# First tile's local scores ahead of its global queries' scores, its operands fetched first in pieces, exponential table loaded at the start

## The chip, the cores and the metric

The kernel runs on one core of one Trainium2 chip. Times are device microseconds (us) of one launch. Before the change the median of three runs is 953.72 us (953.09 to 955.16). The engines are named as in the profile: PE (TensorE matmuls; PEld are its weight loads), DVE (VectorE), ACT (ScalarE), POOL (GpSimd) and SP (SyncE, which here only issues DMAs).

## The reference

Attention for 8 batches of 8 heads, with 512 local and 32 global tokens of 64 dimensions, and then a feed-forward layer over all 8 x 544 rows of 512 features. Global queries see all keys. A local query sees the 32 global keys and the local keys at most 32 places away.

```python
s_g = scale * q_g @ [k_g, k_l].T;   out_g = softmax(s_g) @ [v_g, v_l]
s_ll = where(|i - j| <= 32, scale * q_l @ k_l.T, -1e9)
s_lg = scale * q_l @ k_g.T
out_l = softmax([s_lg, s_ll]) @ [v_g, v_l]
x = concat(out_g, out_l)            # 4352 rows of 512
h = x @ w_in                        # 512 x 2048
g = where(h > 0, h, exp(min(h, 0)) - 1)
out = g @ w_out                     # 2048 x 512
```

## The kernel before

Two generators are interleaved while the program is written: `attention()` and `ffn_stream()`. A third, `load_weights()`, is stepped from the same loop. What a generator writes is then ordered for each engine by a list scheduler, so the order of an engine's instructions is fixed in the program, and every engine works through its own list in order.

**Attention** goes through slots: for each batch `b` and each group `g` of four heads one slot ("g", b, g) for the global queries, and one slot ("l", b, g, t) for each of four tiles `t` of 128 local queries. In batch 0 the order is g0, its tiles 0 to 3, g1, its tiles 0 to 3. The stages of a slot are:

- `stage_ga` (L703 to L732): 16 score matmuls and four small ones of the global queries, two maxima on DVE (L715), their product with the scale (L716), the exponentials on ACT (L720 into `pg`, L722 into `pu`), and two steps later the normalization (`norm`): a sum and a reciprocal on DVE (L726 to L728), then `pk` (four pieces, L731) and `pg` (L732) on POOL.
- `stage_s` (L769 to L795): 8 score matmuls of a local tile, four mask-and-minimum operations on DVE (L780), four exponentials on ACT (L786), and their normalization, a reciprocal on DVE (L791) and four products on POOL (L793). The tile `p` is one of three buffers in turn (p_94, p_95, p_93 in the orders below).
- `stage_t` and `stage_u` (L742 to L811), three slots behind: transposes of `p` (L809), `pz`, `pk` and `pg` on PE, copied into `ptw` and `ptg` by DVE (L811, L753) and ACT (L746 to L750).
- `stage_v` (L822, L853): the products with the values, copied into `xr` by ACT (L859).

Operands are fetched by SP, two slots ahead (`loads`, `AHEAD`): `qg` and two tiles `k` of 640 KB with a "g" slot, two tiles `q` of 256 KB with the first "l" slot, and the mask `msk` behind those.

**Weights.** `unit(m, p, raw)` turns 1 MB of 64-bit weights (`raw`, two buffers, fetched at L174) into two f16 halves: L188 on ACT, L189 on POOL, L193, L196 and L200 on DVE, L204 on ACT, and, after an `all_max` over the partitions (L141, L142), L213 on ACT and L216 on DVE. L204 is the last reader of `raw` as it came; the next fetch into that buffer waits for it.

**Feed-forward.** Its first matmuls (L324) need a block's `xh` and `xl` (L568 on ACT, L571 on DVE), which need that block's whole attention output, and converted weights. Until step 66 of the attention's stages (`PACE`, `lead`) no feed-forward work is written.

At the very start `WARM` matmuls of 512 columns on zeros (L152) keep PE busy while the first operands are on their way. The ACT engine's table of the exponential is loaded where the first exponential is, ahead of L720. The slots of batch 0 before:

```python
slots += [(*a, *t) for g in range(2) for a, t in [(("g", b, g), ())] + [(("l", b, g), (t,)) for t in range(NT)]]
```

Of the kernel before, what the change touches and what calls it, by code (L numbers as in the profile page):

```python
# [10 lines left out]
F32 = mybir.dt.float32  # L11
F32R = mybir.dt.float32r
I32 = mybir.dt.int32
AF = mybir.ActivationFunctionType
# [6 lines left out]
B, H, SL, SG, D = 8, 8, 512, 32, 64  # L21
DM, DF = 512, 2048
P = 128
NT = SL // P
HQ = P // 2
KW = HQ + 3 * 32
# [10 lines left out]
AHEAD = 2  # L37


PACE = ((0, 0), (66, 0), (112, 180), (320, 850))  # L40
WARM = 10
CONV = 14
NBL = B * SL // BLK
GROUPS = {"a": (0, 1), "b": (1, 2), "c": (2, 4), "d": (4, 8), "f": (0, 8)}
# [16 lines left out]
def attn_ffn(ctx: ExitStack, tc: tile.TileContext, qT, qgT, kT, vT, vgT, vpT, w_in, w_out, mask, out):  # L61
    nc = tc.nc
# [3 lines left out]
    wts = ctx.enter_context(tc.tile_pool(name="wts", bufs=1))  # L66
    ffn = ctx.enter_context(tc.tile_pool(name="ffn", bufs=2))
    apool = ctx.enter_context(tc.tile_pool(name="att", bufs=2))
# [33 lines left out]
    msk = wts.tile([P, 3, KW], F32, name="msk")  # L102
# [47 lines left out]
    nc.vector.memset(warm, 0.0)  # L150
    for _ in range(WARM):
        nc.tensor.matmul(ps_o.tile([P, DM], F32, name="acc"), warm[:, 0:P], warm, start=True, stop=True)  # L152
    pww = wts.tile([P, NP], F32, name="pww")
    pwo = wts.tile([P, NP], F32, name="pwo")
    isc = wts.tile([P, NP], F32, name="isc")
    tab = {}

# [502 lines left out]
    def attention():  # L660
# [3 lines left out]
        def load_k(b, hp):  # L664
            k = apool.tile([P, NT, 2, KW], F32, name="k", bufs=4)
            nc.sync.dma_start(k, kT[b, hp])
            return k

        def load_q(b, hp):
            q = apool.tile([P, SL], F32, name="q", bufs=4)  # L670
            nc.sync.dma_start(q, qT[b, hp])
            return q

        def load_qg(b, g):
            qg = apool.tile([P, 2, SG], F32, name="qg", bufs=1)
            nc.sync.dma_start(qg, qgT[b, g])
            return qg
# [235 lines left out]
        slots = []  # L913
        for b in range(B):
            if b == 0:
                slots += [(*a, *t) for g in range(2) for a, t in [(("g", b, g), ())] + [(("l", b, g), (t,)) for t in range(NT)]]
                continue
            body = [("l", b, g, t) for h in range(2) for g in range(2) for t in (2 * h, 2 * h + 1)]
            slots += [("g", b, 0)] + body[:2] + [("g", b, 1)] + body[2:]
        sts = [{"b": b} for b in range(B)]  # L920
        n = len(slots)

        def loads(i):

            s = slots[i]
            st = sts[s[1]]
            if s[0] == "g":
                st["qg", s[2]] = load_qg(s[1], s[2])
                for hp in (2 * s[2], 2 * s[2] + 1):
                    st["k", hp] = load_k(s[1], hp)  # L930
            else:
                for hp in (2 * s[2], 2 * s[2] + 1):
                    if ("q", hp) not in st:
                        st["q", hp] = load_q(s[1], hp)
                if i == 1:
                    nc.sync.dma_start(msk, mask)

        for i in range(AHEAD):
            loads(i)
        def load_values(s):  # L940
            if s and s[0] == "l":
                _, b, g, t = s
                if ("vg", g) not in sts[b]:
                    sts[b]["vg", g] = load_vg(b, g)
                sts[b]["v", g, t] = load_v(b, g, t)
# [3 lines left out]
        for i in range(n + LAGT + 1):  # L949
            if i + AHEAD < n:  # L950
                loads(i + AHEAD)
# [5 lines left out]
            if i == switch:  # L957
                clear(ptw[2])
                k = turns["p"]
# [3 lines left out]
            for what in "SVTU" if i < switch else "TSUV":  # L963
# [7 lines left out]
                elif what == "V":  # L971
                    if pairs:
                        b, g, half = pairs.pop()
# [100 lines left out]
```

## Time and profile before

| | |
|---|---|
| median of three runs | 953.72 us (953.09 to 955.16) |
| the profiled execution's own time | 954.72 us |
| its span on the core | 952.9 us |
| PE / DVE / ACT / POOL busy | 908.5 / 728.1 / 670.1 / 271.1 us |

The span is what the trace covers, from the first to the last instruction. The profiled execution's own time is 1.82 us longer than its span, and 1.00 us above the median. Busy times are sums over the whole span; they are averages over a first part in which no engine is always busy and a long rest in which PE nearly always is.

### The profile page before, as it was taken

What the parts mean: (1) busy time and instruction counts of PE and PEld (TensorE: products, weight loads), DVE (VectorE), ACT (ScalarE), POOL (GpSimd) and SP (SyncE); (2) the same over time, 40 slices, a digit from 0 to 9 for tenths busy, and PEclk for the clock granted to TensorE, in tenths of its full rate; (3) what the DMA queues carried; (4) which work ended last, traced back from release to release, by engine and by line L of the source; (5) the groups of instructions that cost most, each with busy time, mean ns of one, the idle gap of its engine ahead of it and who ended that gap; (6) DMA issues with size and microseconds to landing.
All of it is one profiled execution on the core that took longest, in us unless ns stands there. A gap on an engine that the chain in (4) does not pass through costs nothing.

```text
span 952.9 us, 23830 instructions
## 1 busy us (share of the span) xinstructions
PE 908.5 (95%) x9216; PEld 727.8 (76%) x9216; DVE 728.1 (76%) x2025; ACT 670.1 (70%) x1584; POOL 271.1 (28%) x483
## 2 busy tenths in 40 slices
PE   6889887899999999999999999999999999999997
PEld 3567564566666788888888888888888888888886
DVE  4988988889967777768776877687777777676566
ACT  5888996776656767757677767677767767666564
POOL 4655481461522322122121212221332312100000
PEclk8779999899999999999999999999999999999999
DMA  6855876331342023101330123102310101000000
GB/s 262 299 179 180 282 224 191 124 123 57 115 157 90 23 100 103 47 26 46 105 121 26 46 78 125 47 27 79 122 49 25 46 23 35 2 23 23 1 24 23
DMA packets 41769, 87.64 MB, mean 92 GB/s; under 512 B 7736, under 2 KB 8888, under 8 KB 41656
## 3 DMA queue, kind: packets, MB, share of 16 engines
q1 hardware_dynamic: 41368, 85.85, 26.6%
q8 instruction: 73, 1.20, 0.5%
q14 instruction: 40, 0.33, 0.1%
q10 hardware_dynamic: 288, 0.26, 0.1%
HBM read 70.89 MB, written 15.20 MB: 90 GB/s over the span
## 4 chain that ended last, share of the span: by engine, by line
PE 67%; DVE 14%; ACT 9%; POOL 3%; issue 3%; DMA 3%; SPq 0%; DVEq 0%; ACTq 0%; POOLq 0%
PE pa L324 25%; PE acc L482 12%; PE h L482 9%; PE acc L447 4%; PE pa L822 3%; PE h L324 3%; PE pa L769 3%; PE pa L809 2%; ACT p L786 2%; DMA raw<-w_out 2%; PE pa L889 2%; DVE gl L345 1%; POOL p L793 1%; DVE cu L196 1%; DVE cu L200 1%
## 5 line engine op out<-in xcount | busy, mean ns | idle before, releaser
L324 PEld LDWEIGHTS <-winh 128*128 128x128 f16 x2160 | 209.4, 98 | 39.2 <-issue 8.4
L793 POOL TENSOR_SCALAR p<-p,sm 128x128 f32<-128x128 f32 x256 | 147.8, 593 | 303.2 <-DVE sm L791 165.0
L324 PE MATMUL pa<-xh,winh 128*128 128x256 f16 x824 | 224.9, 273 | 0.1
L324 PE MATMUL pa<-xl,winh 128*128 128x256 f16 x824 | 224.6, 273 | 0.0
L324 PE MATMUL pa<-xh,winl 128*128 128x256 f16 x824 | 224.6, 273 | 0.0
L361 ACT ACTIVATE gh<-gx,xs 128x896 f16<-128x896 f32 x103 | 107.3, 1042 | 123.1 <-DVE gx L358 123.0
L345 DVE SCALAR_TENSOR_TENSOR gl<-gx,xs,gh 128x896 f16<-128x896 f32 x103 | 119.4, 1159 | 59.9 <-ACT gh L361 59.0
L482 PEld LDWEIGHTS <-gh 128*128 128x128 f16 x1456 | 139.5, 98 | 24.0 <-issue 7.4
L786 ACT ACTIVATE p<-p,m 128x160 f32<-128x160 f32 x256 | 106.7, 421 | 41.6 <-DVE m L780 41.4
L324 PEld LDWEIGHTS <-winl 128*128 128x128 f16 x1080 | 106.1, 98 | 14.3 <-issue 1.2
L333 ACT ACTIVATE g<-pa,xs 128x512 f32<-128x512 f32 x103 | 70.3, 682 | 24.4 <-PE pa L324 23.8
L482 PE MATMUL acc<-wouth,gh 128*128 128x256 f16 x312 | 85.2, 273 | 0.0
L482 PE MATMUL acc<-woutl,gh 128*128 128x256 f16 x312 | 85.1, 273 | 0.0
L335 ACT ACTIVATE g<-g 128x512 f32<-128x512 f32 x135 | 85.0, 630 | 0.1
L482 PE MATMUL acc<-wouth,gl 128*128 128x256 f16 x312 | 85.0, 273 | 0.0
L482 PEld LDWEIGHTS <-gl 128*128 128x128 f16 x728 | 71.2, 98 | 9.2 <-DVE gl L345 1.0
L482 PE MATMUL h<-raw,gh 128*128 128x256 f16 x416 | 75.0, 273 | 0.0
L324 PE MATMUL h<-xh,winh 128*128 128x256 f16 x256 | 71.1, 279 | 1.5 <-ACT hs L334 0.9
L324 PE MATMUL h<-xl,winh 128*128 128x256 f16 x256 | 71.0, 278 | 0.7 <-DVE xl L571 0.7
L324 PE MATMUL h<-xh,winl 128*128 128x256 f16 x256 | 71.0, 278 | 0.0
L780 DVE CUSTOM_DVE_ANT_0 p<-pa,msk 128x160 f32<-128x160 f32 x228 | 61.5, 318 | 4.8 <-PE pa L769 4.7
L342 DVE SCALAR_TENSOR_TENSOR gx<-g,hs 128x512 f32<-128x512 f32 x51 | 35.9, 704 | 36.0 <-ACT g L335 35.6
(236 smaller groups left out, 2016.9 us busy)
## 6 DMA issues: line engine op xcount, KB each, us to landing
k<-kT SPq DMA_DIRECT2D x32, 640.0 KB, 5.1
v<-vT SPq DMA_DIRECT2D x64, 256.0 KB, 2.8
q<-qT SPq DMA_DIRECT2D x32, 256.0 KB, 5.6
raw<-w_in SPq DMA_DIRECT2D x8, 1024.0 KB, 5.9
raw<-w_out SPq DMA_DIRECT2D x8, 1024.0 KB, 6.8
out<-o SPq DMA_DIRECT2D x32, 256.0 KB, 2.3
od<-o SPq DMA_DIRECT2D x24, 256.0 KB, 3.1
o<-od SPq DMA_DIRECT2D x24, 256.0 KB, 2.8
```

Of the source, the lines that this page charges most:

```text
L324: nc.tensor.matmul(h[:, j, :], wt[:, c, f], xt[:, c, :], start=k == 0, stop=k == 11)
L333: nc.scalar.activation(g, hf, AF.Relu, scale=sc[:, p:p + 1])
L335: nc.scalar.activation(g, g, AF.Exp, scale=-1.0)
L342: nc.vector.scalar_tensor_tensor(out=out, in0=ins[0], scalar=-1.0, in1=ins[1], op0=ALU.add, op1=ALU.max)
L345: nc.vector.scalar_tensor_tensor(out=dst, in0=src, scalar=sg, in1=hi, op0=ALU.mult, op1=ALU.subtract)
L361: nc.scalar.activation(gh, gx, AF.Copy, scale=sg)
L447: nc.tensor.matmul(acc[t], gt[:, s], wt[:, f, :], start=p == first and j == 0 and k == 0, stop=p == last and j == 1 and k == 2)
L482: nc.tensor.matmul(cols, gt, w, start=p == 0 and k == 0, stop=last and k == len(todo) - 1, skip_group_check=True)
L769: nc.tensor.matmul(sp[r][half * HQ:(half + 1) * HQ, j * KW:(j + 1) * KW], q[rows, qs], k[rows, t, half, :], start=True, stop=True)
L780: nc.vector.tensor_tensor_reduce(out=p, in0=sp[r][:, j * KW:(j + 1) * KW], in1=msk[:, mi, :], op0=ALU.add, op1=ALU.min, scale=-scale, scal ...
L786: nc.scalar.activation(ps[i], ps[i], AF.Exp, bias=m[:, i:i + 1], scale=-1.0, accum_out=s[:, 0, i:i + 1])
L793: nc.gpsimd.tensor_scalar(ps[i][:, 0:P], ps[i][:, 0:P], s[:, 1, i:i + 1], 1.0, ALU.mult, ALU.mult)
```

## The change

The first local tile's slot of batch 0 moves ahead of the first global slot. The operands of these two slots are fetched in a new function: first only those parts of `k`, `q` and the mask that tile 0 reads (160, 64 and 80 KB), the two pieces of `q` from ACT's DMA queue instead of SP's, then `qg`, then the remaining parts. One exponential on a tile of 128 x 1 zeros is written ahead of all else on ACT, so that the table load stands there. Two of the ten warm matmuls go.

```diff
-WARM = 10
+WARM = 8
...
     pwo = wts.tile([P, NP], F32, name="pwo")
+    early = wts.tile([P, 1], F32, name="early")
+    nc.vector.memset(early, 0.0)
+    nc.scalar.activation(early, early, AF.Exp)
...
             if b == 0:
-                slots += [(*a, *t) for g in range(2) for a, t in [(("g", b, g), ())] + [(("l", b, g), (t,)) for t in range(NT)]]
+                slots += [("l", b, 0, 0), ("g", b, 0)] + [("l", b, 0, t) for t in range(1, NT)]
+                slots += [("g", b, 1)] + [("l", b, 1, t) for t in range(NT)]
                 continue
...
-                if i == 1:
-                    nc.sync.dma_start(msk, mask)
-
-        for i in range(AHEAD):
-            loads(i)
+
+        def first_loads():
+
+            st = sts[0]
+            for hp in range(2):
+                k = st["k", hp] = apool.tile([P, NT, 2, KW], F32, name="k", bufs=4)
+                q = st["q", hp] = apool.tile([P, SL], F32, name="q", bufs=4)
+                nc.sync.dma_start(k[:, 0], kT[0, hp][:, 0])
+                nc.scalar.dma_start(q[:, 0:P], qT[0, hp][:, 0:P])
+            nc.sync.dma_start(msk[:, 0, :], mask[:, 0, :])
+            st["qg", 0] = load_qg(0, 0)
+            for hp in range(2):
+                nc.sync.dma_start(st["k", hp][:, 1:], kT[0, hp][:, 1:])
+            for hp in range(2):
+                nc.sync.dma_start(st["q", hp][:, P:], qT[0, hp][:, P:])
+            nc.sync.dma_start(msk[:, 1:, :], mask[:, 1:, :])
+
+        first_loads()
```

The three lines of the table load and the new function push later lines down by 3 and more: in the orders of the changed kernel L789 is the L786 of before, L723 and L725 are L720 and L722, L191 is L188, L192 is L189, L571 is L568, L734 and L735 are L731 and L732, L796 is L793. The scheduler orders all engines anew. From the 140th of ACT's 1268 instructions and the 280th of DVE's 2027 to the end, the orders of before and of the changed kernel are the same.

The start of ACT's list, before:

```order
L720 ACT_TABLE_LOAD
L720 ACTIVATE pg,sg<-pa,mg 128x4x64 x2
L722 ACTIVATE pu,sg<-pa,mg 128x32
L786 ACTIVATE p_94,sm<-p_94,m 128x160 x4
L188 ACTIVATE cu<-raw 128x1024
L786 ACTIVATE p_95,sm<-p_95,m 128x160 x4
L786 ACTIVATE p_93,sm<-p_93,m 128x160 x2
L188 ACTIVATE cu<-raw 128x1024
```

and in the changed kernel:

```order
L947 DMA q<-qT 128x128 x2
L157 ACT_TABLE_LOAD
L157 ACTIVATE early<-early 128x1
L789 ACTIVATE p_94,sm<-p_94,m 128x160 x4
L723 ACTIVATE pg,sg<-pa,mg 128x4x64 x2
L725 ACTIVATE pu,sg<-pa,mg 128x32
L789 ACTIVATE p_95,sm<-p_95,m 128x160 x4
L789 ACTIVATE p_93,sm<-p_93,m 128x160 x2
L191 ACTIVATE cu<-raw 128x1024
```

The local tile's four exponentials stand ahead of the global queries', and the first conversion of weights (L188, now L191) behind six more local exponentials.

POOL's list behind its memsets, before:

```order
L731 TENSOR_SCALAR pk_91<-pu,sg 32x32 x4
L732 TENSOR_SCALAR pg<-pg,sg 128x512
L793 TENSOR_SCALAR p_94<-p_94,sm 128x128 x3
L189 TENSOR_SCALAR cu<-cu 128x1024
L793 TENSOR_SCALAR p_94<-p_94,sm 128x128
L189 TENSOR_SCALAR cu<-cu 128x1024
L793 TENSOR_SCALAR p_95<-p_95,sm 128x128 x4
```

and in the changed kernel:

```order
L796 TENSOR_SCALAR p_94<-p_94,sm 128x128 x4
L734 TENSOR_SCALAR pk_91<-pu,sg 32x32 x4
L735 TENSOR_SCALAR pg<-pg,sg 128x512
L796 TENSOR_SCALAR p_95<-p_95,sm 128x128 x4
L192 TENSOR_SCALAR cu<-cu 128x1024
L796 TENSOR_SCALAR p_93<-p_93,sm 128x128 x4
L192 TENSOR_SCALAR cu<-cu 128x1024
```

Tile 0 is normalized ahead of `pk` and `pg`, and each of the first two weight conversions stands behind one local tile more than before.

ACT's list at the end of the lead, before, from the last tile of group 1 on:

```order
L786 ACTIVATE p_94,sm<-p_94,m 128x160 x2
L859 COPY xr<-h 128x2x128
L786 ACTIVATE p_94,sm<-p_94,m 128x160 x2
L188 ACTIVATE cu<-raw 128x1024
L568 ACTIVATE xh<-xr,xm 128x1024
L720 ACTIVATE pg,sg<-pa,mg 128x4x64 x2
L722 ACTIVATE pu,sg<-pa,mg 128x32
```

and in the changed kernel:

```order
L789 ACTIVATE p_94,sm<-p_94,m 128x160
L571 ACTIVATE xh<-xr,xm 128x1024
L789 ACTIVATE p_94,sm<-p_94,m 128x160
L749 COPY ptw_81<-pa 64x4x32
L751 COPY ptw_81<-pa 64x4x32
L753 COPY ptg_84<-pa 128x2x64
L191 ACTIVATE cu<-raw 128x1024
L723 ACTIVATE pg,sg<-pa,mg 128x4x64 x2
```

The first block's `xh` stood behind the sixth weight conversion (L188, which reads a `raw` that has to arrive) and now stands ahead of it.

## Rows read from the trace of the kernel before

**Rows 1.** The page's first line.
```profile
span 952.9 us, 23830 instructions
```

**Rows 2.** Windows: stretch, length, busy us (count) by engine; clock, DMA share, GB/s.
```profile
10.00:15.00 5.00, 1.11 (x17) 0.78 (x13) 2.93 (x24) 4.99 (x21) 2.32 (x7) 1.00 1.05 403
15.00:20.00 5.00, 4.18 (x23) 2.20 (x23) 2.47 (x4) 3.99 (x16) 3.52 (x5) 0.53 0.68 269
20.00:25.00 5.00, 2.58 (x25) 2.24 (x25) 5.00 (x13) 1.79 (x5) 2.72 (x2) 0.50 0.20 41
250.00:300.00 50.00, 50.00 (x477) 33.94 (x479) 37.51 (x98) 31.82 (x86) 16.95 (x25) 1.00 0.32 108
```

**Rows 3.** Timeline of the first 18 us: start, length, engine, line, [idle before].
```profile
1.18 0.89 SPq L666 DMA_DIRECT2D k<-kT  x2
1.18 4.21 PE L152 MATMUL acc<-wouth 128*128 128x512 f16 x10 [1.18 <-DVE wouth L150]
...
6.84 0.63 PE L703 MATMUL pa<-k,qg 64*32 64x256 f32 x4 [0.39 <-DMA k<-kT]
...
8.76 1.28 ACT L720 ACT_TABLE_LOAD   x1 [8.76 <-DVE mg L716]
9.06 0.33 DVE L780 CUSTOM_DVE_ANT_0 p<-acc,msk 128x160 f32<-128x160 f32 x1 [0.38 <-PE acc L769]
...
10.06 0.47 ACT L720 ACTIVATE pg<-pa,mg 128x256 f32<-128x256 f32 x1
...
11.23 0.43 ACT L786 ACTIVATE p<-p,m 128x160 f32<-128x160 f32 x1
...
12.36 1.37 POOL L731 TENSOR_SCALAR pk<-pu,sg 32x32 f32<-32x32 f32 x4 [8.90 <-ACT p L786]
...
12.88 1.11 ACT L188 ACTIVATE cu<-raw 128x1024 f32<-128x1024 f32 x1
...
14.49 1.07 POOL L793 TENSOR_SCALAR p<-p,sm 128x128 f32<-128x128 f32 x3
...
15.65 1.04 POOL L189 TENSOR_SCALAR cu<-cu 128x1024 f32<-128x1024 f32 x1
...
16.72 0.69 DVE L193 TENSOR_SCALAR cu<-cu 128x1024 int32<-128x1024 int32 x1 [2.86 <-POOL cu L189]
```

**Rows 4.** DMA issues of the first 60 us: line, count, KB each, median us to landing.
```profile
qg<-qgT SPq DMA_DIRECT2D x4, 32.0 KB, 2.5
```

**Rows 5.** Timeline from 18 to 37 us, around the first two conversions of weights.
```profile
18.22 0.69 DVE L811 COPY ptw<-pa 128x512 f32<-128x512 f32 x1 [0.80 <-PE pa L809]
...
22.28 5.09 POOL L793 TENSOR_SCALAR p<-p,sm 128x128 f32<-128x128 f32 x8 [3.50 <-DVE sm L791]
...
24.96 1.16 ACT L204 ACTIVATE raw<-cu 128x1024 f32<-128x1024 f32 x1 [2.20 <-DVE cu L200]
...
26.22 0.38 SPq L174 DMA_DIRECT2D raw<-w_out  x1
...
36.23 1.16 ACT L188 ACTIVATE cu<-raw 128x1024 f32<-128x1024 f32 x1
```

**Rows 6.** Timeline from 63 to 68 us, around the sixth conversion.
```profile
63.05 0.15 DVE L136 TENSOR_SCALAR xm<-xm 128x1 int32<-128x1 int32 x1
64.60 1.13 ACT L188 ACTIVATE cu<-raw 128x1024 f32<-128x1024 f32 x1 [1.61 <-DMA raw<-w_out]
65.63 1.13 ACT L568 ACTIVATE xh<-xr,xm 128x1024 f16<-128x1024 f32 x1
66.67 0.46 ACT L720 ACTIVATE pg<-pa,mg 128x256 f32<-128x256 f32 x1
67.82 1.08 PE L809 MATMUL pa<-ident,p 128*128 128x128 f32 x4 [2.41 <-ACT pg L720]
```

**Rows 7.** Windows of the lead, columns as in rows 2.
```profile
40.00:50.00 10.00, 9.50 (x62) 6.32 (x62) 9.31 (x43) 8.07 (x28) 8.32 (x14) 0.50 0.96 344
50.00:60.00 10.00, 9.88 (x131) 6.95 (x128) 8.33 (x37) 8.42 (x34) 4.64 (x10) 0.86 0.61 192
```

## The prediction

> **What bounds the kernel now.** I read the windows over the whole span first. From 250 us on PE is busy without a gap: 50.00 of 50 us, at the full clock [rows 2]. What stands there is not touched: behind the first seventh of the lists both programs have the same order on every engine. So nothing is won or lost in the long rest; a change of the start reaches the end as a shift, the same number of microseconds at 80 us and at 952.9 us [rows 1]. No transfer in the chain is tied to an absolute time either: the weight fetches wait for buffers, and those shift along.
>
> So the question is when the lead, the first 80 us, is done. There I read the windows of the first 25 us [rows 2]. ACT has no gap from 10 to 15 us (4.99 of 5), while DVE stands half idle (2.93, then 2.47 of 5); from 20 to 25 us it is the other way round: DVE 5.00 of 5, ACT 1.79. The timeline of that stretch [rows 3] says why. ACT does nothing for 8.76 us, since its first work needs the maxima of the global queries' scores, which need 1.3 MB of keys (the landing at 6.84). Then it loads the exponential's table, 1.28 us, and only at 11.23 does the first local exponential start. DVE meanwhile has little to do, and waits 2.86 us ahead of the first weight conversion (L193 at 16.72) for POOL, which stands behind `pk`, `pg` and three products of tile 0. From there DVE, ACT and POOL take turns as the bound.
>
> **The change, part by part.**
>
> *Warm matmuls.* Eight of ten at 4.21 / 10 = 0.42 us [rows 3]: PE is free at 1.18 + 3.37 = 4.55 us. If tile 0's operands are there by then, the cover is gone and nothing is lost.
>
> *Pieces.* Before, the two tiles `k` are issued at 1.18 and the second has landed at 6.84 [rows 3]. Now tile 0 needs 2 x 160 + 2 x 64 + 80 = 528 KB instead of 1312. The smallest transfer of the trace, 32 KB, takes 2.5 us from issue to landing [rows 4]: the mask's piece, SP's third issue (0.45 us for each of the two ahead of it), is issued near 1.7 and so lands at 4.2 at best; going by the old rate, 528 of 1312 KB puts it later by up to 1 us. I take 4.6, PE's own end of the warm-up. One DMA issue more on SP, and two on ACT, lie in time in which both engines had nothing to do.
>
> *Tile 0 first.* With 1 us for its 8 matmuls and one mask operation of 0.33 + 0.08 us, ACT's first local exponential starts near 6.0 instead of 11.23. Four take 1.65 us (11.23 to 12.88 [rows 3]) and end near 7.7. The global queries' keys have 128 KB of `q` and 80 KB of mask ahead of them; of the 6.84 - 1.18 = 5.7 us from issue to landing some 2.5 are the same for any transfer [rows 4], so 1312 KB take 3.2 us and 208 KB 0.5: they land near 7.3. From landing to the maxima took 8.76 - 6.84 = 1.9 us [rows 3]; the global exponentials start near 9.2. Before they did at 10.06, behind the table load: 0.85 us earlier, of which the load gives 1.3 and the later landing takes 0.5.
>
> *The table load.* ACT had 8.76 us without work ahead of it; on the chain it costs 10.06 - 8.76 = 1.30 us [rows 3], and all of that leaves. The Trainium skill, in "ScalarE: Activation LUTs", section "What ACT_TABLE_LOAD costs", counts 1283 ns for the load and about 1380 ns for a drain, 2.66 us in all. By that the global exponentials would start 2.2 us earlier instead of 0.85. The trace has the 1.28 us of the load and an exponential right behind it, so I stay with the row.
>
> *POOL.* Its list now begins with tile 0's four products. A product takes 1.07 / 3 = 0.36 us where DVE is idle and 5.09 / 8 = 0.64 us where DVE is busy [rows 3, 5]. The reciprocal for them comes with the global maxima, near 8.9, so they end between 10.3 and 11.5. `pk` then waits for a DVE reciprocal that stands behind tile 0's copy (0.69 us [rows 5]), the transposes ahead of that, and the global exponentials: between 11.6 and 12.7, where before it was 12.36. I take 12.1. `pk` and `pg` take 14.49 - 12.36 = 2.13 us; then come four products of the next tile (1.4 to 2.5 us) where three stood: the first conversion L189 starts near 16.2 instead of 15.65, and so DVE's L193 near 17.3 instead of 16.72. So the start that was won on ACT, 5 us for the local tile, does not reach the weights: they are about 0.6 us *later*. The second conversion on POOL stands behind four products more, whose reciprocal now stands behind the first conversion on DVE. That opens a wait of some 1.5 us on DVE that it did not have (5.00 of 5 in 20 to 25 us [rows 2]): the second L204, at 24.96 before [rows 5], comes near 26.5, 1.6 us late.
>
> But more is done by then. Going down both lists to the second L200, DVE has behind it, beyond what it had before, three mask operations (0.33 each), tile 1's copy to `ptw` (0.69), 1.7 us by these rows [rows 3, 5], and two small reductions and a `pz`, which I put at half of that, an estimate: about 2.4 us. ACT has, up to the second L204, three local exponentials (1.24) and four copies more. 2.4 us of work done, 1.6 us late: **0.8 us gained**. Bounds: 2.4 if POOL's products all run at 0.36 and nothing is late; nothing at all, or a little below, if all run at 0.64.
>
> The fetch of the fourth `raw` moves to about 27.8 from 26.22; it was used at 36.23, ten us later [rows 5], so 1.6 us are covered there. Were that cover gone, the 1.6 us would be lost.
>
> *The sixth conversion.* At 62.99 ACT waits 1.61 us for `raw`, converts (64.60), then makes `xh` of the first block (65.63) and only then the global exponentials (66.67), for which PE waits 2.41 us [rows 6]. What `xh` needs was ready at 63.05 + 0.15. Now `xh` stands ahead of the wait, in time that was idle, and the exponentials follow the conversion at once: 66.67 - 65.63 = **1.04 us**. Bounds: 0, if `raw` comes so early that the order makes no difference, and 1.6.
>
> *Sum.* 0.8 + 1.04 = 1.8 us. The profiled execution goes from 954.72 to 952.9 us; it lies 1.00 above the median, so the same shift of the median gives **951.9 us**. All shorter or longer terms are bounded by 0 and 2.4 + 1.6 = 4.0 us.
>
> **The rivals.** About 0.2% (1.9 us) is what a measurement of this kernel can tell from no change.
>
> *The head start is given back.* If weights, and not DVE's or ACT's work in all, set the end of the lead, then the 2.4 us of work done early are idle later, and the 0.6 and 1.6 us of lateness count: with the 1.04 us behind them, a gain of 0 +- 0.8, 953.7 us. For it: L193 waits on POOL for 2.86 us now. Against: DVE is at 9.31 of 10 us from 40 to 50 [rows 7], where work done early is worth its time. The same time comes out if the pieces land no earlier than the whole tiles did. Chance 0.19.
>
> *More, by the clock.* From 40 to 50 us PE is granted half its clock (0.50, that is 1.2 GHz) and is busy 9.50 of 10 us [rows 7]. If the shifted work leaves it at 2.4 GHz there, DVE with 9.31 of 10 is the bound, which frees 0.7 us, and of DVE's 1.7 idle us in 50 to 60 us another 1.5, some 2.2 us in all: 1.8 + 2.2 = 4.0 us, 949.7 us. Chance 0.18.
>
> *Slower, by the clock.* PE works 9.88 of 10 us from 50 to 60 us, at 0.86 [rows 7]. If the half-clock stretch moves there, each us of it costs half a us, since PE has no slack. Eleven us, about as long as the stretch it has now, cost 5.5 us: 951.9 + 5.5 = 957.4 us. It turns the sign when it covers 3.6 us and is seen as slower from 7.4 us on. That fewer warm matmuls can start it is in the Trainium skill, "TensorE: Matmul & The Clock Gate", section "What's actually happening": the default state is throttled, and activity releases it. By that rule a later release would also put tile 0's scores and the global queries' at half speed, some 1 us of the gain. The rows bear it out in part: the warm matmuls, 0.42 us for 512 columns, run at 1.2 GHz. Chance 0.13.
>
> **How the numbers follow.** The forecast, a gain of 0.8 to 3 us (950.7 to 952.9), has 0.50; 0.27 of it lies beyond 1.9 us, 0.23 within. Faster: 0.27 + 0.18 = 0.45. Same: 0.23 + 0.18 of the first rival's 0.19, 0.41. Slower: 0.13 and the last hundredth, 0.14. The range leaves out a tenth at each end: down to 948.0 (beyond the 4.0 us of the clock rival) and up to 956.0, inside the slower rival.
>
> **What would show it.** ACT's first local exponential near 6 us; table load before 3 us; global exponentials near 9.2; L193 (now L196) at 17.3 rather than 16.7; the second L204 (now L207) near 26.5; `xh` ahead of the sixth conversion, and the first feed-forward matmul 1.8 us earlier than its place before; from there a constant shift. Wrong would be made of it by a different half-clock stretch between 40 and 75 us, or by a first conversion that is not late, so that 2 us more are won.

## The result and the profile after

The changed kernel takes 955.58 us (median of 22 runs, 952.33 to 959.27), the kernel before, run beside it, 952.31 us (22 runs, 948.46 to 958.29). The ratio of the comparison is 1.0047, 95% interval 1.0031 to 1.0063, about 4.5 us (the two medians alone lie 3.3 us apart): **slower** by half a per cent, with an interval clear of 1, where 1.8 us of gain were forecast. Single runs of one program differ by some 10 us, so a single span decides nothing here. The page of the changed kernel has a shorter span than [rows 1], because that run lay low among its own and that of before lay high:

```profile
span 951.9 us, 23838 instructions
```

So for differences late in the lead I compare two further profiles that lie at their kernels' medians, e1_before (span 949.2) and e12_after_again (953.9). Up to the first feed-forward matmul the weight conversions of the two profiles of before agree within 0.5 us, those of the two of the changed kernel within 1.6: in e12_after_again four of the first global score matmuls take 1.07 us instead of 0.63 in the first profile after, and the global exponentials start at 11.13 instead of 10.38.

The timeline of the first 18 us of the changed kernel answers to [rows 3]:

```profile
1.64 0.43 SPq L948 DMA_DIRECT2D msk<-mask  x1
1.66 1.28 ACT L157 ACT_TABLE_LOAD   x1 [1.66 <-PEq L1082]
2.12 0.43 SPq L679 DMA_DIRECT2D qg<-qgT  x1
2.59 0.91 SPq L951 DMA_DIRECT2D k<-kT  x2
...
6.00 0.43 ACT L789 ACTIVATE p<-p,m 128x160 f32<-128x160 f32 x1 [2.85 <-DVE m L783]
...
8.42 0.63 PE L706 MATMUL pa<-k,qg 64*32 64x256 f32 x4 [0.39 <-DMA k<-kT]
...
10.30 1.47 POOL L796 TENSOR_SCALAR p<-p,sm 128x128 f32<-128x128 f32 x4 [6.83 <-DVE mg L719]
10.38 0.47 ACT L723 ACTIVATE pg<-pa,mg 128x256 f32<-128x256 f32 x1 [2.62 <-PE pa L772]
...
13.16 1.36 POOL L734 TENSOR_SCALAR pk<-pu,sg 32x32 f32<-32x32 f32 x4 [1.39 <-DVE sg L731]
...
16.79 1.04 POOL L192 TENSOR_SCALAR cu<-cu 128x1024 f32<-128x1024 f32 x1
...
17.86 0.69 DVE L196 TENSOR_SCALAR cu<-cu 128x1024 int32<-128x1024 int32 x1 [0.34 <-POOL cu L192]
```

The local exponential starts at 6.00, as forecast. The rest of the keys does not land near 7.3 but at 8.42: SP issues the mask's piece at 1.64 and `qg` at 2.12, and comes to the keys' rest at 2.59, where it issued the whole tiles at 1.18 before. The global exponentials thus start at 10.38, *later* than the 10.06 of before, and POOL's list is about 0.8 us later than it was.

From 18 to 30 us (answers to [rows 5]):

```profile
20.00 2.51 POOL L796 TENSOR_SCALAR p<-p,sm 128x128 f32<-128x128 f32 x4 [2.17 <-DVE sm L794]
...
22.59 1.04 POOL L192 TENSOR_SCALAR cu<-cu 128x1024 f32<-128x1024 f32 x1
...
23.67 0.69 DVE L196 TENSOR_SCALAR cu<-cu 128x1024 int32<-128x1024 int32 x1 [1.46 <-POOL cu L192]
...
27.46 1.13 ACT L207 ACTIVATE raw<-cu 128x1024 f32<-128x1024 f32 x1 [2.29 <-DVE cu L203]
```

The wait of 1.46 us on DVE is the forecast one, but the second L207, the step that frees the buffer `raw`, comes at 27.46 instead of 24.96: 2.5 us late, not 1.6.

Windows, columns as in [rows 2]; the second and third answer to [rows 7], the last to the end of [rows 2]:

```profile
20.00:25.00 5.00, 2.43 (x11) 1.73 (x13) 3.51 (x9) 3.13 (x8) 4.83 (x7) 0.50 0.28 52
...
40.00:50.00 10.00, 7.87 (x99) 6.53 (x100) 8.67 (x38) 8.99 (x35) 5.42 (x12) 0.89 0.95 325
50.00:60.00 10.00, 7.98 (x111) 5.36 (x107) 9.99 (x47) 9.04 (x30) 5.82 (x11) 1.00 0.84 283
...
250.00:300.00 50.00, 50.00 (x495) 34.06 (x497) 37.50 (x97) 32.89 (x88) 15.88 (x25) 1.00 0.36 115
```

From 20 to 25 us POOL is now full (4.83 of 5) and DVE is not (3.51, before 5.00). From 40 to 60 us PE runs faster than before (0.89 and 1.00 against 0.50 and 0.86) and yet nothing is gained: it is busy only 7.87 and 7.98 of 10 us.

### The profile page after: what moved, and what is told of

The parts are those of the page before. It is cut to its first block, busy times and chain, and to the rows that moved or that the text cites. A ratio compares the mean times of both kernels' runs of the same rounds, so it can differ in the third digit from the quotient of the medians.

```text
span 951.9 us, 23838 instructions
## 1 busy us (share of the span) xinstructions
PE 903.6 (95%) x9214; PEld 725.6 (76%) x9214; DVE 728.4 (77%) x2026; ACT 670.7 (70%) x1585; POOL 271.1 (28%) x483
## 3 DMA queue, kind: packets, MB, share of 16 engines
q1 hardware_dynamic: 41800, 85.72, 26.7%
## 4 chain that ended last, share of the span: by engine, by line
PE 69%; DVE 13%; ACT 10%; issue 3%; DMA 2%; POOL 2%; SPq 0%; DVEq 0%; ACTq 0%; POOLq 0%
PE pa L327 25%; PE acc L485 12%; PE h L485 9%; PE acc L450 4%; PE h L327 4%; PE pa L825 4%; PE pa L772 3%; PE pa L812 3%; ACT p L789 2%; PE pa L892 2%; DVE gl L348 1%; PE pa L706 1%; ACT cu L191 1%; DVE xl L574 1%; ACT g L336 1%
## 5 line engine op out<-in xcount | busy, mean ns | idle before, releaser
L327 PEld LDWEIGHTS <-winh 128*128 128x128 f16 x2160 | 209.2, 98 | 39.4 <-issue 8.7
L796 POOL TENSOR_SCALAR p<-p,sm 128x128 f32<-128x128 f32 x256 | 143.4, 578 | 309.3 <-DVE sm L794 163.7
L327 PE MATMUL pa<-xh,winh 128*128 128x256 f16 x824 | 224.9, 273 | 0.1
L327 PE MATMUL pa<-xl,winh 128*128 128x256 f16 x824 | 224.6, 273 | 0.0
L327 PE MATMUL pa<-xh,winl 128*128 128x256 f16 x824 | 224.6, 273 | 0.0
L364 ACT ACTIVATE gh<-gx,xs 128x896 f16<-128x896 f32 x103 | 107.3, 1042 | 123.3 <-DVE gx L361 123.2
L789 ACT ACTIVATE p<-p,m 128x160 f32<-128x160 f32 x256 | 106.8, 420 | 44.5 <-DVE m L783 44.3
L327 PEld LDWEIGHTS <-winl 128*128 128x128 f16 x1080 | 106.0, 98 | 14.3 <-issue 1.3
L338 ACT ACTIVATE g<-g 128x512 f32<-128x512 f32 x135 | 85.1, 630 | 0.1
L327 PE MATMUL h<-xh,winh 128*128 128x256 f16 x256 | 70.7, 278 | 1.8 <-ACT hs L337 1.0
L327 PE MATMUL h<-xl,winh 128*128 128x256 f16 x256 | 70.9, 277 | 0.8 <-DVE xl L574 0.8
L327 PE MATMUL h<-xh,winl 128*128 128x256 f16 x256 | 70.9, 277 | 0.0
```

What stands on the lines that cost most here:

```text
L327: nc.tensor.matmul(h[:, j, :], wt[:, c, f], xt[:, c, :], start=k == 0, stop=k == 11)
L338: nc.scalar.activation(g, g, AF.Exp, scale=-1.0)
L364: nc.scalar.activation(gh, gx, AF.Copy, scale=sg)
L789: nc.scalar.activation(ps[i], ps[i], AF.Exp, bias=m[:, i:i + 1], scale=-1.0, accum_out=s[:, 0, i:i + 1])
L796: nc.gpsimd.tensor_scalar(ps[i][:, 0:P], ps[i][:, 0:P], s[:, 1, i:i + 1], 1.0, ALU.mult, ALU.mult)
```

## The experiments

Four theories stand in the expectations. **A (order):** the second weight conversion comes late, because more local-tile work stands ahead of it on POOL and ACT, and its lateness is handed on through the two buffers `raw` to the end of the lead. **B (clock):** PE is granted 1.2 GHz elsewhere, because fewer warm matmuls and different gaps lie ahead. **C (landing):** the pieces make the global keys land later, and all behind them. **D (end of the lead):** the late start is made good by 65 us and the loss arises where `xh` stands ahead of the sixth conversion.

All numbers in one place. Ratios are to the kernel before, run beside each. The starts, in us, come from one profile each: of the second and fourth release (L204, in the changed kernel L207: the step that frees a buffer `raw`), of the first feed-forward matmul (L324, L327) and of the first feed-forward activation (L335, L338), for which 24 of these matmuls must be done.

| run | median | ratio, 95% | 2nd | 4th | first L324 | first L335 |
|---|---|---|---|---|---|---|
| first profile before | 952.31 | | 25.0 | 47.4 | 77.1 | 81.1 |
| first profile after | 955.58 | 1.0047 [1.0031, 1.0063] | 27.5 | 50.4 | 78.3 | 82.2 |
| e1_before | 950.75 | 1.0003 [0.9985, 1.0020] | 24.9 | 47.9 | 76.7 | 80.7 |
| e2_table | 949.72 | 0.9996 [0.9982, 1.0009] | 25.3 | 48.2 | 76.3 | 80.2 |
| e3_oldslots | 955.58 | 1.0056 [1.0035, 1.0076] | 26.8 | 50.4 | 81.4 | 86.3 |
| e4_whole | 956.50 | 1.0061 [1.0039, 1.0082] | 29.2 | 52.0 | 80.7 | 84.7 |
| e5_warm10 | 956.17 | 1.0051 [1.0029, 1.0074] | 27.7 | 50.4 | 78.3 | 84.0 |
| e6_clamp3 | 955.23 | 1.0048 [1.0023, 1.0073] | 29.2 | 51.3 | 80.7 | 84.8 |
| e7_after_noclamp | 957.39 | 1.0073 [1.0050, 1.0096] | 25.0 | 49.5 | 79.6 | 85.3 |
| e8_before_noclamp | 958.46 | 1.0080 [1.0056, 1.0105] | 24.6 | 50.7 | 80.5 | 84.6 |
| e9_conv_first | 954.79 | 1.0049 [1.0029, 1.0069] | 27.7 | 52.0 | 81.0 | 86.4 |
| e10_conv_x | 955.73 | 1.0066 [1.0047, 1.0085] | 28.1 | 50.9 | 80.0 | 85.1 |
| e11_whole_early | 952.14 | 1.0017 [1.0001, 1.0033] | 27.4 | 49.9 | 78.7 | 82.7 |
| e12_after_again | 955.67 | 1.0053 [1.0034, 1.0073] | 28.2 | 50.8 | 78.6 | 84.2 |
| e13_copies | 952.63 | 1.0030 [1.0017, 1.0043] | 26.7 | 48.1 | 76.5 | 82.1 |
| e14_copies_dve | 950.65 | 1.0006 [0.9985, 1.0027] | 25.3 | 46.7 | 76.5 | 80.5 |
| e15_table_dve | 953.10 | 1.0023 [1.0008, 1.0038] | 24.2 | 47.6 | 77.4 | 81.4 |
| e16_copies_dve2 | 951.76 | 1.0008 [0.9992, 1.0025] | 26.2 | 48.0 | 77.5 | 81.4 |

**The two kernels again** (e1 unchanged before, e12 unchanged after):

> The kernel of before once more, for a second trace of it and for what two identical programs differ by. Theory A (order): the changed kernel is slower because the second weight conversion stands behind tile 2's products on POOL and comes 2.5 us late, which the lead never makes up; then here the second L204 stands within 0.3 us of 24.96 again, and the ratio is 1.000 within 0.002. Theory B (clock): the difference between the two programs is which stretches PE spends at half clock, and those differ by execution; then this trace has other half-clock stretches, and the start of the feed-forward stage moves by more than 1 us against the first trace.

> The changed kernel again, unchanged, beside the three above: a second profile of it, and its time on the same chip. All theories: 1.003 to 1.006 of the kernel before. If half-clock stretches near 80 and 107 us belong to its order, both profiles have them; the first has the one at 107.1 only.

The loss is there again. The two also show how lateness travels. ACT's timeline from 24 to 52 us, conversions alone, in e1_before:

```profile
24.93 1.15 ACT L204 ACTIVATE raw<-cu 128x1024 f32<-128x1024 f32 x1 [2.20 <-DVE cu L200]
...
28.60 1.13 ACT L188 ACTIVATE cu<-raw 128x1024 f32<-128x1024 f32 x1
...
37.52 1.14 ACT L204 ACTIVATE raw<-cu 128x1024 f32<-128x1024 f32 x1
...
47.91 1.15 ACT L204 ACTIVATE raw<-cu 128x1024 f32<-128x1024 f32 x1 [1.18 <-DVE cu L200]
```

and in e12_after_again:

```profile
28.21 1.16 ACT L207 ACTIVATE raw<-cu 128x1024 f32<-128x1024 f32 x1 [1.43 <-DVE cu L203]
...
30.37 1.15 ACT L216 ACTIVATE winh<-cu,cm 128x1024 f16<-128x1024 f32 x1 [0.93 <-DVE cm L136]
...
32.73 1.14 ACT L216 ACTIVATE wouth<-cu,cm 128x1024 f16<-128x1024 f32 x1
33.77 1.12 ACT L191 ACTIVATE cu<-raw 128x1024 f32<-128x1024 f32 x1
...
40.40 1.16 ACT L207 ACTIVATE raw<-cu 128x1024 f32<-128x1024 f32 x1
...
49.31 1.18 ACT L191 ACTIVATE cu<-raw 128x1024 f32<-128x1024 f32 x1 [1.02 <-DMA raw<-w_in]
50.77 1.15 ACT L207 ACTIVATE raw<-cu 128x1024 f32<-128x1024 f32 x1 [0.28 <-DVE cu L203]
```

Both L216 need the maximum that the releases collect, so they are late too; ACT works in order, and the third L191 stands behind both of them in the changed list (33.77 against 28.60). The third release follows at 40.40 instead of 37.52 (the third conversion is not alone in this: ACT's list also waits for PE ahead of it, 2.50 us at 39.10). The fetch into its buffer waits for it, so the conversion at 49.31 now waits 1.02 us for its data, a wait that the list of before did not have at that place. The fourth release is 2.9 us late, the first feed-forward matmul 1.9 us, the first L338 3.5 us, the span 4.7 us. The lateness is absorbed only in part; why it grows again behind the first matmul is read under B.

**One part at a time.** e2 puts the early table load alone on the kernel before; e3 gives the changed kernel the old slot order; e4 gives it whole tiles, on SP alone (keys, queries, mask, `qg`); e5 gives it ten warm matmuls.

```diff
 # e2, on before
+    early = wts.tile([P, 1], F32, name="early")
+    nc.vector.memset(early, 0.0)
+    nc.scalar.activation(early, early, AF.Exp)
 # e3, on after
-                slots += [("l", b, 0, 0), ("g", b, 0)] + [("l", b, 0, t) for t in range(1, NT)]
-                slots += [("g", b, 1)] + [("l", b, 1, t) for t in range(NT)]
+                slots += [(*a, *t) for g in range(2) for a, t in [(("g", b, g), ())] + [(("l", b, g), (t,)) for t in range(NT)]]
 # e4, on after, in first_loads
-                nc.sync.dma_start(k[:, 0], kT[0, hp][:, 0])
...
+                st["k", hp] = load_k(0, hp)
...
+                st["q", hp] = load_q(0, hp)
+            nc.sync.dma_start(msk, mask)
+            st["qg", 0] = load_qg(0, 0)
 # e5, on after
-WARM = 8
+WARM = 10
```

> Before, with the early table load alone. The global exponentials start at 8.8 instead of 10.06 us. Theory A: the first two conversions keep their places on POOL (behind tile 0, and behind tile 1), so the second L204 comes at 25 to 26 us, not at 27.5, and the time is that of before or up to 1.3 us less: ratio 0.998 to 1.001. Theory C (keys): what costs is the later landing of the global queries' keys, 8.42 instead of 6.84; here they land as before, and the ratio is below 1.000. By neither is it slower.

> The changed kernel with the slots of batch 0 in the old order; pieces, early table load and eight warm matmuls stay. The scheduler then puts the second conversion on POOL right behind the first, ahead of tile 2's products. Theory A: the second L204 comes near 25 us, 2 us or more ahead of the changed kernel's 27.46, and the time falls by 2 to 3 us, ratio to before 0.999 to 1.002. Theory C: the keys still land at 8.4, and the time stays that of the changed kernel, ratio 1.004 to 1.006.

> The changed kernel with whole tiles fetched (k, k, q, q, mask, qg on SP), so that tile 0 still goes first but waits for all of its operands; table load, slots and eight warm matmuls stay. On POOL the first conversion then stands right behind tile 0's products and the second behind pk and pg. Theory A: conversions come early, the second L204 at 25 us or sooner, ratio at or below 1.001. Theory C: the keys land near 7 and it is faster than the changed kernel too, but by the 1.4 us of the landing alone. Theory B: as slow as the changed kernel, 1.003 to 1.006.

> The changed kernel with ten warm matmuls again instead of eight; all else as changed. Theory A (the loss is the second conversion of weights, whose second weight cast to raw, L207, ends late because POOL and ACT have more local work ahead of it): that cast still starts near 27 us, and the time stays 3 to 6 us above the kernel before. Theory B (the loss is the clock: two warm matmuls less, or work begun earlier, puts PE's half-clock stretches where they cost more): with the old warm-up the stretches go back to where the kernel before has them, and the time comes within 1.5 us of it.

In e2 the table load is off the chain and the global exponentials start 1.1 us earlier than in e1_before (10.01):

```profile
0.72 1.28 ACT L157 ACT_TABLE_LOAD   x1 [0.72 <-PEq L1067]
...
8.91 0.47 ACT L723 ACTIVATE pg<-pa,mg 128x256 f32<-128x256 f32 x1 [6.69 <-DVE mg L719]
```

It gains nothing that can be told from no change. e3 and e5 lose as much as the change: the loss needs neither the new slot order nor the two warm matmuls that went (e3 comes out as C expected and not as A did). e4 loses it without the pieces, against A's expectation. So no single part carries it: with pieces and with whole tiles, with either order, the second release comes between 26.8 and 29.2. e4 does not yet rule out C, since its global exponentials start late too (11.40; their scores wait for `qg`); e14 below does, which keeps the pieces and their later landing and loses nothing.

**Making one conversion late, or early.** e6 does the second unit's clamp (L189, one POOL instruction) three times in the kernel before; e7 and e8 leave it out, after and before.

```diff
 # e6, on before
-            nc.gpsimd.tensor_scalar(u, u, FMAX, FMIN, ALU.min, ALU.max)
+            for _ in range(3 if (m, p) == (1, 0) else 1):
+                nc.gpsimd.tensor_scalar(u, u, FMAX, FMIN, ALU.min, ALU.max)
 # e7 on after, e8 on before
+            if (m, p) != (1, 0):
+                nc.gpsimd.tensor_scalar(u, u, FMAX, FMIN, ALU.min, ALU.max)
```

> The kernel before, with the clamp of the second weight conversion (L189 on POOL, about 1.04 us) written three times over; the result is the same, and only this one conversion comes later. Theory A: the second L204 moves from 24.9 us to about 27 to 28, as in the changed kernel, and the time rises by 2.5 to 5 us. Theory B: nothing of the start is otherwise changed, so the stretches stay and the time is within 1.5 us of the kernel before.

> The changed kernel without the clamp of the second weight conversion (1 of 16 MB of weights goes unclamped). Theory A: its casts and shifts need POOL no more, the second L207 comes at 25 to 26.5 us instead of 27.5, and 1 to 3 us of the 4.5 us loss are back. Theory B: no difference to the changed kernel, 3 to 6 us above the kernel before.

> The control for the run above: the kernel before without the clamp of the second weight conversion (1 of 16 MB of weights goes unclamped). Theory A: the second L204 comes 0.5 to 1.5 us earlier than 24.9 us, and the time is 0 to 2 us below the kernel before. Theory B: no difference to the kernel before.

e6 makes the second release 4.3 us late. The scheduler moves the later steps of the conversion, and what stands beside them, back with it; from about 46 us on the orders of ACT, DVE and POOL are those of before. The first feed-forward matmul is 4.0 us late, and the kernel before loses as much as by the whole change (1.0048 against 1.0047):

```profile
17.75 3.21 POOL L190 TENSOR_SCALAR cu<-cu 128x1024 f32<-128x1024 f32 x2
...
23.12 1.04 POOL L190 TENSOR_SCALAR cu<-cu 128x1024 f32<-128x1024 f32 x1
...
29.23 1.14 ACT L205 ACTIVATE raw<-cu 128x1024 f32<-128x1024 f32 x1
```

That lateness made in the first 46 us, around this conversion, suffices is thus shown. e7 and e8 missed: A expected a gain from each. With one instruction less the scheduler orders the lists anew. In e7 the second release is on time (25.0), but the third L191 is 3.4 us and the fourth 5.1 us later than in e1_before; in e8 the second is early (24.6) and the fourth release 2.8 us late. So A in its simple form, the second release alone, falls. What all kernels from 1.0047 up share is a late *fourth* release, whatever made it late: at 46.7 to 48.2 the ratios are 0.9996 to 1.0030, from 49.5 on 1.0047 to 1.0080. But it does not decide alone: e11 has it late (49.9) at 1.0017, and e13 loses 0.30% with the release of e2 (48.1 and 48.2).

**The end of the lead.** In the changed kernel `xh` stands ahead of the sixth conversion. The timeline from 63 us on answers to [rows 6]:

```profile
63.38 0.43 ACT L789 ACTIVATE p<-p,m 128x160 f32<-128x160 f32 x1 [1.40 <-DVE m L783]
...
64.94 1.14 ACT L571 ACTIVATE xh<-xr,xm 128x1024 f16<-128x1024 f32 x1
...
67.11 1.12 ACT L191 ACTIVATE cu<-raw 128x1024 f32<-128x1024 f32 x1
68.12 0.47 ACT L723 ACTIVATE pg<-pa,mg 128x256 f32<-128x256 f32 x1
```

The global exponentials come at 68.12 where they were at 66.67. e9 puts the sixth conversion ahead of `xh` again; e10 also moves the second block's `xh` back.

```diff
 # e9, on after
+            with tc.high_priority(offset=400 if (m, p) == (1, 2) else 0):
                 nc.scalar.activation(u, high.bitcast(F32), AF.Abs)
 # e10, on e9
+                with tc.high_priority(offset=-100 if blk == 1 else 0):
                     nc.scalar.activation(hf, xf, AF.Copy, scale=mx[:, 4:5])
```

> The changed kernel with one more instruction moved: the sixth conversion's L191 on ACT ahead of the first block's xh again, as before; the rest of the lists is as changed. Theory D (the changed kernel makes its late start good by 65 us, and loses where the lead ends: the conversion behind xh and four more instructions holds POOL, whose next products PE waits for): 0.5 to 1.5 us faster than the changed kernel, near 954.5. The prediction's own term (xh ahead of the conversion is worth 1.04 us): 1 us slower than the changed kernel, near 956.6. Theory A (only the second L207 counts): no difference, 955.6.

> The same, and the second block's xh behind the three copies of a tile's transposes instead of between them; PE waited 1.2 us for the last of these copies at 72.7 us in the changed kernel. Theory D: that wait goes, another 0.5 to 1.2 us, near 953.5. Theory A and a theory of the clock alone: no difference to the changed kernel, 955.6.

Neither helps (1.0049 and 1.0066), so D falls as the cause of the loss; a gain of a microsecond would hide in the intervals. By then the lead is late whatever stands first: the fourth release is at 52.0 and 50.9.

**Taking the lateness away.** In e4 the second L191 stands on ACT behind three copies of tile 0's transposes, which wait for PE:

```profile
19.63 0.26 ACT L749 COPY ptw<-pa 64x128 f32<-64x128 f32 x1 [3.43 <-PE pa L748]
...
21.19 1.14 ACT L191 ACTIVATE cu<-raw 128x1024 f32<-128x1024 f32 x1
```

e11 moves these copies of the first tile back in e4, e13 does so in the changed kernel, e14 also gives the second unit's clamp to DVE, and e16 the first unit's too.

```diff
 # e11 on e4, e13 on after
+            with tc.high_priority(offset=-400 if (st['b'], g, t) == (0, 0, 0) else 0):
                 nc.scalar.copy(pt[0:HQ, 0, 32:] ...
 # e14, on e13 (e16: nc.vector if p == 0)
-            nc.gpsimd.tensor_scalar(u, u, FMAX, FMIN, ALU.min, ALU.max)
+            (nc.vector if (m, p) == (1, 0) else nc.gpsimd).tensor_scalar(u, u, FMAX, FMIN, ALU.min, ALU.max)
```

> The kernel with whole tiles fetched (local tile first, table early, eight warm matmuls; it was 1.0061 of the kernel before, its second L191 stood behind the first tile's copies L749 to L753 on ACT, and its second L207 came 4.3 us late), with these copies behind the second L191 instead. Theory A for this family: the second L207 comes at 25 to 26.5 us instead of 29.2, and most of the 4 to 5 us are back: within 1.5 us of the kernel before. Theory of the clock alone: still 3 to 6 us slower than it.

> The changed kernel with one thing moved: the first tile's three copies L749 to L753 on ACT are given a low priority, as in the run before. The second L191 comes two instructions earlier on ACT, and the lists at the end of the lead fall back into the order of the kernel before (sixth conversion, xh, global exponentials, both tiles' copies). POOL's list is as changed. Theory A with carry (what is late at the second L207 is carried through the fourth and to the end; the order at the end of the lead adds 1 to 3 us): the second L207 about as late as in the changed kernel or 1 us less (26.5 to 27.5 us), that lateness carried unchanged from 27 to 135 us, no half-clock stretch near 107 to 113; 1.0020 to 1.0035 of the kernel before. If the end of the lead costs nothing: 1.005, as the changed kernel.

> The same, and the clamp of the second weight conversion done by DVE instead of POOL (about 0.7 us more on DVE; POOL's products of a local tile stood ahead of it). Theory A with carry: the second L207 another 0.5 to 1.5 us earlier, at 25.5 to 26.5, and the time with it, 1.000 to 1.002 of the kernel before. If POOL's queue is not what makes it late: as the run above or 0.7 us slower.

> As e14, with the first conversion's clamp on DVE too. DVE idles 2.28 us ahead of 16.40 us in e14, and the first L196 waits for POOL: if both weight conversions follow, the second L207 comes 0.5 to 1 us earlier than in e14 (25.3), and the time is 949 to 950; if it is the local tile's four masks that DVE waits for there, no difference to e14, 950.7.

e11 brings e4's ratio from 1.0061 to 1.0017, some 4 of 5.8 us, and its first matmul from 80.7 to 78.7; e13 brings the change's from 1.0053 to 1.0030, nearly half of its loss (the two intervals overlap), and its first matmul from 78.6 to 76.5. In e13 the end of the lead, too, falls back into the order of before; but at the fourth release, ahead of that, 2.7 us of the lateness are already gone. The second release is still late in e13, behind POOL:

```profile
18.77 3.44 POOL L797 TENSOR_SCALAR p<-p,sm 128x128 f32<-128x128 f32 x4 [0.91 <-DVE sm L795]
...
22.29 1.04 POOL L192 TENSOR_SCALAR cu<-cu 128x1024 f32<-128x1024 f32 x1
...
26.71 1.14 ACT L207 ACTIVATE raw<-cu 128x1024 f32<-128x1024 f32 x1 [2.14 <-DVE cu L203]
```

Tile 2's products hold the clamp up. e14 takes it off POOL:

```profile
21.18 0.68 DVE L192 TENSOR_SCALAR cu<-cu 128x1024 f32<-128x1024 f32 x1
...
25.29 1.18 ACT L207 ACTIVATE raw<-cu 128x1024 f32<-128x1024 f32 x1 [0.94 <-DVE cu L203]
```

and the whole loss is gone (1.0006, interval 0.9985 to 1.0027), with every part of the change still in. The earlier release is not what shows at the end, though: the first feed-forward matmul starts at 76.5 in e13 and e14, and at 76.7 in e1_before. What parts e13 from the other two behind that is the clock (see B). e16 adds nothing.

Is that a gain of its own, which any kernel would have had? e15 puts the same clamp on DVE, with the early table, in the kernel before (on e2, the `+` line of e14).

> The control for e14 and a candidate to beat both: the kernel before with the table loaded early, and the second conversion's clamp on DVE instead of POOL; slots, fetches and warm matmuls as before. If POOL's queue costs the second L204 time in the kernel before as well, it comes 0.5 to 1 us earlier than 24.9 us, and the time is 0.5 to 1.5 us below the kernel before; if DVE is the bound there (5.00 of 5 us from 20 to 25 us), the 0.7 us of the clamp make it 0 to 0.7 us later, and the time 0 to 1 us longer.

It does not gain: the second release is 0.7 us earlier than in e1_before (24.2), the first matmul 0.7 us later, and the kernel 0.23% slower; whether by the 0.68 us more work on DVE or by the new order was not separated. So the remedy is no gain of its own; it helps the changed kernel, where the clamp was late. No version beats the kernel before beyond what can be told apart.

**B, the clock.** The condition of the rival on the good side came true (0.89 and 1.00 from 40 to 60 us) and gave nothing. Behind the lead, though, the clock takes a part of the loss. The first and the last start of the 24 matmuls ahead of the first L335, in e1_before

```profile
76.71 0.27 PE L324 MATMUL h<-xh,winh 128*128 128x256 f16 x1
...
79.22 0.27 PE L324 MATMUL h<-xh,winl 128*128 128x256 f16 x1
```

and in e12_after_again

```profile
78.58 0.38 PE L327 MATMUL h<-xh,winh 128*128 128x256 f16 x1
...
82.76 0.27 PE L327 MATMUL h<-xh,winl 128*128 128x256 f16 x1
```

From the first to the last it takes 2.51 us in the one and 4.18 in the other, where PE is granted 1.2 GHz from 78.6 to 82.0. So of the 3.5 us at the first L338 1.9 are the lead's and 1.7 the clock's. In e13 the second part stands alone: the first matmul is not late, but the first L338 is, by 1.4 us. Windows from 75 to 80 us, in e13_copies

```profile
75.00:80.00 5.00, 4.94 (x25) 3.37 (x26) 4.29 (x17) 2.71 (x13) 3.97 (x7) 0.66 0.00 0
```

and in e14_copies_dve

```profile
75.00:80.00 5.00, 5.00 (x66) 4.04 (x65) 4.95 (x21) 4.69 (x20) 3.31 (x5) 1.00 0.22 54
```

A half-clock stretch slows these matmuls in the profiles of e3, e5, e7, e9, e10, e12 and e13, and in none of the others; the first profile of the changed kernel, one of its faster executions, has none there either.

Later the kernels differ once more. Windows from 105 to 115 us, in e1_before

```profile
105.00:115.00 10.00, 10.00 (x115) 6.14 (x112) 9.08 (x41) 9.50 (x28) 6.17 (x16) 1.00 0.97 326
```

and in e12_after_again

```profile
105.00:115.00 10.00, 7.80 (x74) 5.21 (x72) 9.69 (x28) 8.38 (x26) 2.96 (x5) 0.83 0.86 265
```

PE is busy only 7.80 us there, and 3.4 us of the stretch are granted 1.2 GHz (109.3 to 112.7). In e4_whole it is no busier, but at the full clock:

```profile
105.00:115.00 10.00, 7.80 (x90) 4.55 (x90) 10.00 (x29) 9.44 (x27) 3.48 (x6) 1.00 0.89 314
```

From the first to the seventh L335 it takes 54.9 or 55.0 us in the first profile of before, e1, e2, e4 and e11, none of which has a half-clock stretch there, and 55.3 to 59.3 us in the two of the changed kernel and the other runs, each of which has one. It arises between the fourth and the fifth L335, 27.7 us in e1, 27.9 in e11 and e14, 30.7 and 31.6 in the two of the changed kernel; a part is made up again by the seventh. The sum of such stretches does not tell it: over the whole span the mean granted clock is 0.981 in e12 and 0.979 in e1, whose longest stretches lie in the lead.

So B holds as a second term. How large the two terms are can only be estimated. e11's first matmul is 2.0 us late and e6's 4.0, and they lose some 1.6 and 4.5 us; by that the changed kernel's, 1.1 us late between the first profiles and 1.9 between e12 and e1, is worth 1 to 2.5 of the 4.5 us. e13, with no lateness there and both stretches (76.6 to 80.0 and 107.3 to 110.8), loses 2.9 us; e14, whose stretch (100.7 to 104.1) lies elsewhere, nothing. No edit set the clock by itself: e13 was expected to lose the stretch near 107 and kept it. Whether the order of the lists brings the stretches or chance does, and how the loss in the medians splits, stays open.

## Why the prediction was wrong

*Right:* tile 0's operands at about 4.6, the first local exponential at 6.00, POOL's order, the wait opened on DVE (1.46, forecast 1.5), and a long rest from 250 us on that is not touched (50.00 of 50 us). Right in kind but 0.6 us short: the first L192 at 16.79 and L196 at 17.86 (forecast 16.2 and 17.3).

*Failed, first: "the later landing takes 0.5".* The step priced the extra pieces by their bytes. What delayed the keys was their place on SP: they are issued at 2.59 instead of 1.18, behind issues of 0.43 us each, and land 1.58 us later than before (8.42 against 6.84). That takes all of the 1.30 that the table load gave up: the global exponentials are not 0.85 us earlier but 0.32 later. The Trainium skill, "ScalarE: Activation LUTs", section "What ACT_TABLE_LOAD costs", would have put 2.66 us on the load; with the load off the chain (e2) the exponentials start 1.1 us earlier, close to the 1.30 of the row, so its drain is not seen here. What is more, e2 shows that not even this is worth anything that can be told at the end.

*Failed, and this one turned the sign: "2.4 us of work done, 1.6 us late: 0.8 us gained".* The lateness was mis-sized (2.5 us in the first profile after, 3.3 between e12 and e1), and no credit against it shows: the first feed-forward matmul starts 1.1 to 1.9 us later than before, not 1.8 earlier. Work done early on DVE and ACT is worth its time only if these engines' work in all sets the end of the lead. From 20 to 25 us it does not: DVE, full before, is busy 3.51 of 5 and POOL 4.83. What the runs show in its place is the sequence of conversions through two buffers, in the fixed order of ACT, DVE, POOL and SP. A second release 4.3 us late makes the first matmul 4.0 us late and the kernel slower by about 4.5 (e6); a first matmul that is not late, and at the full clock, goes with no loss (e14); a second release that is early wins nothing (e15). The rival "the head start is given back" had this mechanism and even its ground, and I gave it 0.19. It took the lateness as 0.6 and 1.6 us against a gain of 1.04, which made it no change instead of a loss.

*Failed: "the fetch of the 4th `raw` is covered".* For the fetch that was looked at that holds, but the lateness travels on ACT as well, by the third L191 behind both L216, and reaches a fetch without cover (the wait of 1.02 us at 49.31 in e12).

*Failed: "1.04 us" for the sixth conversion.* The step left ACT's start of that stretch where it was. ACT waits 1.40 us for DVE at 63.38 and has three copies more ahead of the conversion; the global exponentials come 1.45 us later, not 1.04 earlier, and the order itself makes no difference that can be told (e9).

*Failed: "nothing is won or lost in the long rest", "a constant shift".* The sum put PE's clock behind 80 us at nothing, with no reason but that the lists are the same there. From the first to the seventh L335 the lateness of e4 (4.0) and e11 (2.0) is carried unchanged, and 1.0 to 1.6 us of it are made up by the 25th; in e12 3.5 us at the first, 1.7 of them the clock's, become 6.2 at the seventh and 4.7 in the span. So what is lost at 80 us does reach the end for the greater part, but half-clock stretches up to 140 us add to it, by the estimate above some half of the loss.

*The slower rival by the clock*, at 0.13, had the right term in the wrong place: its half-clock stretch from 50 to 60 us is not there (1.00), those near 78 and 107 us are. Its other half, first scores at half speed, is there in e12 (1.07 us for four matmuls) and not in the first profile after (0.63).

## What to carry to other kernels

Work done early is a gain only if the engine that does it sets the end of the stage (here neither DVE nor ACT did); find the sequence that does (here conversions through two buffers), and price a move by what it does to that sequence alone, each instruction ahead of it on every in-order list included. When a transfer is cut into pieces, count the issues ahead of the last piece that the chain needs, not the bytes. And where a scheduler orders the lists, an edit of one instruction reorders many: taking one clamp away made this kernel 0.8% slower, so a single removal is no clean experiment until its order has been read. When a later stage starts late, read also at what clock it runs: a mark behind its first matmuls mixes the two.

## What the hardware showed that I had not expected

POOL slows down beside DVE more than my bound of 0.64 us for a product. Four 128x128 products take 1.41 to 1.47 us where DVE does small operations, and 3.44 us in e13 (0.86 each) beside DVE's 128x1024 shifts; in e2

```profile
16.55 4.04 POOL L796 TENSOR_SCALAR p<-p,sm 128x128 f32<-128x128 f32 x4 [0.52 <-DVE sm L794]
```

they take 4.04, 1.0 each. It goes the other way too, in e12_after_again, on DVE and POOL:

```profile
19.21 0.16 DVE L793 TENSOR_SCALAR sm<-sm 128x4 f32<-128x4 f32 x1
...
23.19 1.10 POOL L192 TENSOR_SCALAR cu<-cu 128x1024 f32<-128x1024 f32 x1
...
23.32 1.00 DVE L793 TENSOR_SCALAR sm<-sm 128x4 f32<-128x4 f32 x1
```

DVE's operation on four columns takes 0.16 us at 19.21 and 1.00 us when it starts just behind POOL's clamp: it ends with it. The Trainium skill, "SBUF — State Buffer", section "Who interferes with whom", has DVE and GpSimd share a pair of ports as an exclusive lock: where a DVE instruction uses that pair, the one that comes second is blocked for the whole instruction. These rows agree with that; no run here was made to isolate it.

Two profiles of one program also differ in where PE is granted half its clock: between 75 and 140 us the first profile of the changed kernel has one stretch (107.1 to 110.5), e12_after_again three of them (at 78.6 until 82.0, 109.3 until 112.7 and 133.2 until 136.6).
